# Causal attention before two feed-forward layers: the third and fourth unit's scores in one run, both value products behind them

## The chip, the cores and the metric

The kernel runs on one core of one Trainium2 chip. Its time is the device time of one execution in microseconds. Three runs of the kernel before gave 975.97, 975.77 and 975.14 us, median 975.77 us. A profile, taken in a run of its own, is where all readings below come from.

## The reference

An attention with a causal mask and a bias that only decays (4 batches, 8 heads, 576 positions, head size 64) feeds two feed-forward layers (2304 tokens, width 512, inner width 2048). All in float32; the inputs are scaled so that single-pass products would not do.

```python
scores = scale * np.matmul(q, k.transpose(0, 1, 3, 2))      # 4 x 8 heads, 576 x 576
cum = np.cumsum(np.maximum(s, 0.0), axis=-1)
bias = -(cum[:, :, :, None] - cum[:, :, None, :])
scores = np.where(causal, -1e9, scores + np.minimum(bias, 0.0))
attn = np.exp(scores - scores.max(-1, keepdims=True))
attn = attn / (attn.sum(-1, keepdims=True) + 1e-09)
x = np.matmul(attn, v)                                       # -> 2304 x 512
h = x @ w_in;  x = np.maximum(0.01 * h, h) @ w_out           # first layer
h = x @ w2_in; out = softplus(h) @ w2_out                    # second layer
```

## The kernel before

Two heads that lie side by side in the 128 partitions make a **pair**; there are 16 pairs (0 to 15), four to a batch. A pair is cut into four **units** of score rows, in this order: the first unit is rows 384 to 511 of both heads (512 keys each), the second the 64 last rows of both heads ("last" in the code, two stretches of 288 keys), the third rows 256 to 383 (384 keys), the fourth rows 128 to 255 and 0 to 127 (256 and 128 keys). A loop over 64 + 3 **steps** runs them: step i (0 to 3) of a pair is written as `p, i = divmod(n, 4)`, and in it `u0` is the unit whose softmax starts, `u1` the one before it, `u2` the one before that. For a unit the stations are

- scores on TensorE (`scores`, L311 and, for the second unit, L297), one step ahead of its own: `start(n + 1)`. They use half of the array's rows for each head. They fill a bank of PSUM for each half (tags `s0` and `s1`, two banks each, so units take turns);
- in its own step maxima on VectorE (`maxima`, L332) and exponentials on ScalarE (`exps`, L344), first half `j = 0`, second half `j = 1`;
- one step later the sums' reciprocals on VectorE (L350, L351) and the scaling on GpSimd (`norm`, L355);
- two steps later the transposes on TensorE (`transpose`, L372, L367, L363; three or four of 128 x 128 in a half) into one of two banks (tag `t`), and the copies out of them (`evacuate`, L384 on ScalarE, L386 on VectorE) to the tiles PA, PZ and PB. A transpose waits for the copy out of the bank two halves earlier.

The second product (`pv`, L403) of pair p - 1 stands in pair p: at the end of step 0 that for its rows 384 to 575, a bank with 192 columns out of PA and PZ; at the end of step 2 that for rows 0 to 383, out of PB. It uses half of the array's columns for each head. Its result is split in two parts, `xh` on ScalarE (L410) and `xl` on VectorE (L414).

Between these stand **fill units**: pieces of the first feed-forward layer for a batch that is done, to give TensorE work while the softmax runs. A fill unit is twelve matmuls of 512 columns with the whole array (L145 or L614), six in one step and six in the next, into a single bank (tag `m`). When the twelve are done, ScalarE copies them out of the bank (L587 or L618, written at the end of the second step), and the next unit's first matmul waits for that. From pair 7 to pair 10 a fill unit begins in steps 0 and 2; step 0 of pair 11 has none, and from there on they begin in steps 1 and 3 (step 1 of pair 15 has none). The weights for it are prepared in the same steps (`split_w`: two copies on ScalarE at L108 and L109, then L114, L117, L120 on VectorE, L123 on GpSimd, L127 on ScalarE, L133 on GpSimd).

All engines work through their instructions in the order in which the program writes them; `later(k, f)` writes f after k ticks, with one tick in the middle and one at the end of each step. The attention ends at about 240 us; what follows is the two feed-forward layers alone.

Of the kernel before, what the change touches and what calls it, by code (L numbers as in the profile page):

```python
# [10 lines left out]
F32 = mybir.dt.float32  # L11
# [3 lines left out]
AF = mybir.ActivationFunctionType  # L15
ALU = mybir.AluOpType
PSUM = bass.MemoryType.PSUM

P = 128
# [12 lines left out]
def attn_moe_moe(ctx, tc, q, k, v, s, w1i, w1o, w2i, w2o, out):  # L32
    nc = tc.nc

    B, H, S = s.shape
    D = v.shape[-1]
# [5 lines left out]
    NPAIR = H // 2  # L42
# [26 lines left out]
    def later(n, fn, *args):  # L69
        todo.setdefault(clock[0] + n, []).append((fn, args))  # L70
# [84 lines left out]
    def attention(att, ps, fills):  # L155
# [232 lines left out]
        def pv(p, last):  # L388
# [12 lines left out]
            for m, (c, x, o, w) in enumerate(mms):  # L401
                for j in range(2):
                    nc.tensor.matmul(  # L403
                        pt[j * D:(j + 1) * D, o:o + w], V[p % 2][:, c, j, :], x[:, j, :],
                        start=m == 0 or (not last and m == 1), stop=m == len(mms) - 1 or (not last and m == 0),
                    )
            c = slice(b * S + q0, b * S + q0 + n)

            def high():
                nc.scalar.activation(xh[:, hp, c], pt[:, :n], AF.Copy)  # L410
                later(1, low)

            def low():
                nc.vector.tensor_tensor(xl[:, hp, c], pt[:, :n], xh[:, hp, c].bitcast(F32), op=ALU.subtract)  # L414
                if not last and hp == NPAIR - 1 and b < B - 1:
                    fill.ready(b)

            later(1, high)

        mask = att.tile([P, NB * P], F32, tag="mask", name="mask")  # L420
        maskl = att.tile([P, S // 2], F32, tag="maskl", name="maskl")
# [33 lines left out]
        order = [[NB - 1], [], [NB - 2], [1, 0]]  # L455
        units = [(p, ts) for p in range(NP) for ts in order]
        live = {}

        def start(n):
            if n < len(units):  # L460
                live[n] = Unit(*units[n])
                live[n].scores()

        start(0)
        for n in range(len(units) + 3):
            p, i = divmod(n, len(order))
            u0, u1, u2, u3 = (live.get(n - d) for d in range(4))
            if u3:
                u3.evacuate(1)
            start(n + 1)  # L470
            if u0:
                u0.maxima(0)
                u0.exps(0)
            if u1:
                u1.divisors()
                u1.norm(0)
            if u2:
# [12 lines left out]
                fill.step(n)  # L490
            if u0:
                u0.maxima(1)
            if u2 and u0 and u0.last:
                u2.evacuate(0)
            if u0:
                u0.exps(1)
# [7 lines left out]
            if u1:  # L504
                u1.norm(1)
            if u2:
                if not (u0 and u0.last):
                    u2.evacuate(0)
                u2.transpose(1)
            if i == 3 and p + 1 < NP:  # L510
                load(p + 1, "v")
            elif i in (0, 2) and p:
                pv(p - 1, i == 0)
            if n >= len(units):
                fill.run()
# [335 lines left out]
```

## Time and profile before

| | |
|---|---|
| median of three runs | 975.77 us |
| the profiled execution | 976.11 us |
| its span in the trace | 974.3 us |
| TensorE (PE) busy | 967.0 us, 5268 matmuls |
| weight loads (PEld) busy | 785.0 us |
| VectorE (DVE) / ScalarE (ACT) / GpSimd (POOL) busy | 529.3 / 536.1 / 576.2 us |
| chain that ended last | PE 97% |
| PE in its chain at L311, L403, L372 | 5%, 4%, 4% |
| granted TensorE clock | 9 (0.9 or more) in each of the forty slices |

The profile's own time is 1.8 us longer than its span, and 0.34 us above the median of the runs. Times in the rows below are microseconds from the start of the span. A matmul row gives the start and the length of a merged group; the ends are modelled and overlap, so differences are taken from start to start. A float32 matmul shows as two records (two passes), and the two heads' matmuls start 0.007 us apart and run side by side in their halves of the array.

### The profile page before, as it was taken

The numbers are of one execution on the slowest core, as the hardware profiler recorded it, in microseconds if no ns is written. First come the engines' busy times: TensorE is split into PE (matmuls) and PEld (weight loads), VectorE is DVE, ScalarE is ACT, GpSimd is POOL, SyncE is SP. The second block draws the span as 40 slices with busy tenths as digits, with TensorE's granted clock in tenths as the row PEclk, the third lists the DMA queues.
The fourth block names the chain that finished last, engine by engine and source line by source line (L and its number), as shares of the span: only waits on it lengthen the run. The fifth ranks groups of instructions, "written<-read, shape, count | busy, mean of one in ns | idle before, by whom it ended". The sixth has DMA issues, their size and how long they took to land.

```text
span 974.3 us, 14738 instructions
## 1 busy us (share of the span) xinstructions
PE 967.0 (99%) x5268; PEld 785.0 (81%) x5268; DVE 529.3 (54%) x1140; ACT 536.1 (55%) x1119; POOL 576.2 (59%) x568
## 2 busy tenths in 40 slices
PE   9999999999999999999999999999999999999998
PEld 6666777777998888888888888888888888888886
DVE  7888566554122222222325358666688868764434
ACT  6888677565453333333344456766656655654452
POOL 7788556443454444344535556777677767774554
PEclk9999999999999999999999999999999999999999
DMA  6444452420621111111102110211011101100202
GB/s 230 156 160 140 134 170 77 143 73 23 218 85 43 44 44 43 35 52 44 44 23 65 44 44 22 65 39 48 22 44 45 64 23 44 44 0 1 87 22 87
DMA packets 37774, 68.06 MB, mean 70 GB/s; under 512 B 3018, under 2 KB 20298, under 8 KB 37700
## 3 DMA queue, kind: packets, MB, share of 16 engines
q1 hardware_dynamic: 37268, 66.36, 21.2%
q8 instruction: 42, 0.69, 0.3%
q10 hardware_dynamic: 432, 0.75, 0.2%
q14 instruction: 32, 0.26, 0.1%
HBM read 59.01 MB, written 8.09 MB: 69 GB/s over the span
## 4 chain that ended last, share of the span: by engine, by line
PE 97%; DVE 1%; POOL 1%; ACT 0%; issue 0%; DMA 0%; DVEq 0%; POOLq 0%
PE ps_h L145 41%; PE ps_out L752 37%; PE pt_s L311 5%; PE pt_v L403 4%; PE pt_t L372 4%; PE ps_o L614 3%; PE pt_t L367 1%; PE pt_s L297 1%; PE pt_w L191 0%; POOL sc L355 0%; DVE sc L332 0%; POOL wil L133 0%; DVE acc L764 0%; DVE PA L386 0%; ACT sc L344 0%
## 5 line engine op out<-in xcount | busy, mean ns | idle before, releaser
L151 POOL TENSOR_TENSOR gl<-gf,gh 128x512 fp32r<-128x512 f32 (+2 forms) x148 | 182.6, 1234 | 150.5 <-ACT gh L150 140.8
L145 PE MATMUL ps_h<-xh,wih 128*128 128x512 f32 (+2 forms) x640 | 237.5, 371 | 0.0
L145 PE MATMUL ps_h<-xh,wil 128*128 128x512 f32 (+2 forms) x640 | 235.8, 368 | 0.0
L145 PE MATMUL ps_h<-xl,wih 128*128 128x512 f32 (+2 forms) x640 | 235.6, 368 | 0.0
L764 DVE TENSOR_TENSOR acc<-ps_out,acc 128x512 f32<-128x512 f32 (+1 forms) x115 | 73.8, 657 | 164.2 <-PE ps_out L752 164.2
L711 POOL TENSOR_TENSOR t<-e,t 128x512 f32<-128x512 f32 (+1 forms) x80 | 112.2, 1403 | 72.2 <-DVE t L710 71.4
L355 POOL TENSOR_SCALAR sc<-sc,st 128x512 f32<-128x512 f32 (+4 forms) x160 | 89.0, 567 | 82.7 <-DVE st L351 76.2
L145 PEld LDWEIGHTS ps_h<-xh,wil 128*128 128x128 f32 x640 | 120.5, 188 | 19.7
L145 PEld LDWEIGHTS ps_h<-xh,wih 128*128 128x128 f32 x640 | 120.6, 188 | 19.3
L145 PEld LDWEIGHTS ps_h<-xl,wih 128*128 128x128 f32 x640 | 120.6, 189 | 19.1
L695 ACT ACTIVATE gf<-ps_h 128x512 f32<-128x512 f32 (+2 forms) x68 | 37.3, 548 | 177.4 <-PE ps_h L145 174.6
L150 ACT ACTIVATE gh<-gf 128x512 fp32r<-128x512 f32 (+2 forms) x148 | 86.1, 582 | 49.1 <-DVE gf L721 48.5
L752 PE MATMUL ps_out<-woh,gl 128*128 128x512 f32 x289 | 112.5, 389 | 0.0
L752 PE MATMUL ps_out<-wol,gh 128*128 128x512 f32 x289 | 112.4, 389 | 0.0
L752 PE MATMUL ps_out<-woh,gh 128*128 128x512 f32 x289 | 112.4, 389 | 0.0
L123 POOL TENSOR_TENSOR wm<-wm,wt 128x512 int32<-128x512 int32 x64 | 85.2, 1332 | 30.7 <-DVE wm L120 30.7
L344 ACT ACTIVATE sc<-sc,st 128x512 f32<-128x512 f32 (+2 forms) x144 | 83.4, 583 | 31.4 <-DVE st L350 20.1
L752 PE MATMUL ps_out<-gh,wol 128*128 128x512 f32 (+2 forms) x272 | 99.1, 364 | 0.0
L752 PE MATMUL ps_out<-gh,woh 128*128 128x512 f32 (+2 forms) x272 | 99.1, 364 | 0.0
L752 PE MATMUL ps_out<-gl,woh 128*128 128x512 f32 (+2 forms) x272 | 99.0, 364 | 0.0
L710 DVE TENSOR_SCALAR t<-e 128x512 f32<-128x512 f32 (+1 forms) x80 | 44.2, 552 | 98.2 <-ACT e L701 98.2
L114 DVE TENSOR_SCALAR wm<-wm 128x512 f32<-128x512 f32 x64 | 38.1, 596 | 92.7 <-ACT wm L108 92.6
(112 smaller groups left out, 1677.1 us busy)
## 6 DMA issues: line engine op xcount, KB each, us to landing
rawi<-in_moe_w_in SPq DMA_DIRECT2D x32, 512.0 KB
rawo<-in_moe_w_out SPq DMA_DIRECT2D x32, 512.0 KB
K<-in_k SPq DMA_DIRECT2D x15, 432.0 KB
V<-in_v SPq DMA_DIRECT2D x16, 320.0 KB
Q<-in_q SPq DMA_DIRECT2D x15, 320.0 KB
out<-acc SPq DMA_DIRECT2D x17, 256.0 KB
M<-c_d SPq DMA_DIRECT2D x30, 144.0 KB
part<-o SPq DMA_DIRECT2D x12, 256.0 KB
```

Of the source, the lines that this page charges most:

```text
L123: nc.gpsimd.tensor_tensor(m, m, t, op=ALU.add)
L145: nc.tensor.matmul(ps, a, b, start=kk == 0 and n == 0, stop=kk == KD - 1 and n == 2)
L150: nc.scalar.activation(gh, gf, AF.Copy)
L151: nc.gpsimd.tensor_tensor(gl, gf, gh.bitcast(F32), op=ALU.subtract)
L311: nc.tensor.matmul(self.ps[j][:, c], x[r, t * P:(t + 1) * P], y[r, :(t + 1) * P], start=x is Q[i], stop=x is bq,)
L344: nc.scalar.activation(x, x, AF.Exp, scale=-1.0, bias=self.stat(0, e + self.last), accum_out=self.stat(1, e))
L355: nc.gpsimd.tensor_scalar(x, x, self.stat(2, e), 1.0, op0=ALU.mult, op1=ALU.mult)
L372: nc.tensor.transpose(pt[:, c * P:(c + 1) * P], sc[:, j, c * P:(c + 1) * P], ident)
L710: nc.vector.tensor_scalar(t, e, 1.0, -1.0, op0=ALU.add, op1=ALU.add)
L711: nc.gpsimd.tensor_tensor(t, e, t, op=ALU.subtract)
L752: nc.tensor.matmul(u, a, v, start=f == 0 and m == 0, stop=f == G - 1 and m == 2 and j == k - 1)
L764: nc.vector.tensor_tensor(d[..., x], o[..., x], d[..., x], op=ALU.add)
```

## The change

From pair 7 to pair 15 the second step's `start(n + 1)` is left out: the third unit's scores are issued at the head of step 2, and the fourth unit's right behind them. Behind these stands `pv2`, which does both second products of pair p - 1 in one run: first the one out of PB, then the one out of PA and PZ. Its 576 columns don't fit a bank of 512, so each matmul of 192 columns is parted into one of 128 (same bank as the rest) and one of 64, which goes to free columns of the third unit's score bank. The two products at the end of steps 0 and 2 are gone for these pairs. `finish` writes the two parts of the result: for the 64 columns L414 and L421 of the new file at the end of step 2, for the other 512 in one instruction each, ScalarE's at the end of step 2 and VectorE's in the middle of step 3. In step 2 the second unit's reciprocals and first scaling now come before the third unit's maxima; in step 0 the copy out of the third unit's first transposes (`evacuate(0)`) now comes before the exponentials of the second half. For each pair 26 matmul instructions take the place of 18 in the second product.

```diff
--- before.py
+++ after.py
@@ -404,18 +404,42 @@
                         pt[j * D:(j + 1) * D, o:o + w], V[p % 2][:, c, j, :], x[:, j, :],
                         start=m == 0 or (not last and m == 1), stop=m == len(mms) - 1 or (not last and m == 0),
                     )
+            finish(p, pt[:, :n], q0, n, 1, not last)
+
+        def finish(p, pt, q0, n, wait, end):
+            b, hp = divmod(p, NPAIR)
             c = slice(b * S + q0, b * S + q0 + n)
 
             def high():
-                nc.scalar.activation(xh[:, hp, c], pt[:, :n], AF.Copy)
-                later(1, low)
+                nc.scalar.activation(xh[:, hp, c], pt, AF.Copy)
+                if n == TL:
+                    low()
+                else:
+                    later(1, low)
 
             def low():
-                nc.vector.tensor_tensor(xl[:, hp, c], pt[:, :n], xh[:, hp, c].bitcast(F32), op=ALU.subtract)
-                if not last and hp == NPAIR - 1 and b < B - 1:
+                nc.vector.tensor_tensor(xl[:, hp, c], pt, xh[:, hp, c].bitcast(F32), op=ALU.subtract)
+                if end and hp == NPAIR - 1 and b < B - 1:
                     fill.ready(b)
 
-            later(1, high)
+            later(wait, high)
+
+        def pv2(p, rest):
+
+            pt = ps.tile([P, 512], F32, tag="a", name="pt_v", bufs=1)
+            q3, qt = pt[:, SB - P:], rest[:, SB - P:SB - P + TL]
+            mms = [(0, PB[:, :, 2, :P], pt[:, :P], True, True)] + [
+                (c, PB[:, :, c, max(0, c - 1) * P:], pt[:, max(c, 1) * P:SB - P], c == 0, c == NB - 2)
+                for c in range(NB - 1)
+            ]
+            for c in range(NB):
+                mms += [(c, PA[:, :, c, :P], q3, c == 0, c == NB - 1), (c, PA[:, :, c, P:], qt, c == 0, False)]
+            mms.append((NB, PZ, qt, False, True))
+            for c, x, y, a, z in mms:
+                for j in range(2):
+                    nc.tensor.matmul(y[j * D:(j + 1) * D], V[p % 2][:, c, j, :], x[:, j, :], start=a, stop=z)
+            finish(p, qt, SB, TL, 2, False)
+            finish(p, pt, 0, SB, 2, True)
 
         mask = att.tile([P, NB * P], F32, tag="mask", name="mask")
         maskl = att.tile([P, S // 2], F32, tag="maskl", name="maskl")
@@ -455,9 +479,10 @@
         order = [[NB - 1], [], [NB - 2], [1, 0]]
         units = [(p, ts) for p in range(NP) for ts in order]
         live = {}
+        wide = 7
 
         def start(n):
-            if n < len(units):
+            if n < len(units) and n not in live:
                 live[n] = Unit(*units[n])
                 live[n].scores()
 
@@ -467,11 +492,21 @@
             u0, u1, u2, u3 = (live.get(n - d) for d in range(4))
             if u3:
                 u3.evacuate(1)
-            start(n + 1)
+            late = wide <= p < NP
+            if late and i == 2:
+                start(n)
+                u0 = live[n]
+            if not late or i != 1:
+                start(n + 1)
+            if late and i == 2:
+                pv2(p - 1, u0.ps[0])
+            if u1 and late and i == 2:
+                u1.divisors()
+                u1.norm(0)
             if u0:
                 u0.maxima(0)
                 u0.exps(0)
-            if u1:
+            if u1 and not (late and i == 2):
                 u1.divisors()
                 u1.norm(0)
             if u2:
@@ -490,7 +525,8 @@
                 fill.step(n)
             if u0:
                 u0.maxima(1)
-            if u2 and u0 and u0.last:
+            soon = u2 and u0 and (u0.last or late and i == 0)
+            if soon:
                 u2.evacuate(0)
             if u0:
                 u0.exps(1)
@@ -504,12 +540,12 @@
             if u1:
                 u1.norm(1)
             if u2:
-                if not (u0 and u0.last):
+                if not soon:
                     u2.evacuate(0)
                 u2.transpose(1)
             if i == 3 and p + 1 < NP:
                 load(p + 1, "v")
-            elif i in (0, 2) and p:
+            elif i in (0, 2) and p and not late:
                 pv(p - 1, i == 0)
             if n >= len(units):
                 fill.run()
```

TensorE, pair 13, from the third unit's second transposes (step 0) to the first fill matmul of step 1, before. The rows name line, operation, result and operands, the shape, and the engines waited for.

```order
L372 MATMUL pt_t<-ident,sc 128x128 [waits DVE_49,Pool_49]
L372 MATMUL pt_t<-ident,sc 128x128 x2
L403 MATMUL pt_v<-PA,V_97 64x192 [waits DMAHW5_49]
L403 MATMUL pt_v<-PA,V_97 64x192 x7
L403 MATMUL pt_v<-PZ,V_97 64x64 x2
L311 MATMUL pt_s<-K_88,Q_86 128x384 [waits DVE_49] x2
L311 MATMUL pt_s<-BK_92,BQ_90 128x384 x2
L372 MATMUL pt_t<-ident,sc 128x128 [waits Activation_49,Pool_49]
L372 MATMUL pt_t<-ident,sc 128x128
L372 MATMUL pt_t<-ident,sc 128x128 [waits Pool_49]
L145 MATMUL ps_h<-xh,wih 128x512 [waits Activation_49]
```

The same stretch after:

```order
L372 MATMUL pt_t<-ident,sc 128x128 [waits DVE_49,Pool_49]
L372 MATMUL pt_t<-ident,sc 128x128 x2
L372 MATMUL pt_t<-ident,sc 128x128 [waits Activation_49,Pool_49]
L372 MATMUL pt_t<-ident,sc 128x128
L372 MATMUL pt_t<-ident,sc 128x128 [waits Pool_49]
L145 MATMUL ps_h<-xh,wih 128x512 [waits Activation_49]
```

The second product (L403) and the third unit's scores (L311) are gone from between the two groups of three transposes, so the fourth unit's first transposes (they wait for ScalarE and GpSimd) and the fill's first matmul (it waits for ScalarE) follow at once.

TensorE, pair 13, the end of step 1 and the head of step 2, before:

```order
L372 MATMUL pt_t<-ident,sc 128x128 x3
L311 MATMUL pt_s<-K_88,Q_86 128x256 x2
L311 MATMUL pt_s<-BK_92,BQ_90 128x256 x2
L311 MATMUL pt_s<-K_88,Q_86 128x128 x2
L311 MATMUL pt_s<-BK_92,BQ_90 128x128 x2
L372 MATMUL pt_t<-ident,sc 128x128 x4
```

The same place after, up to the second matmul of 64 columns:

```order
L372 MATMUL pt_t<-ident,sc 128x128 x3
L311 MATMUL pt_s<-K_88,Q_86 128x384 x2
L311 MATMUL pt_s<-BK_92,BQ_90 128x384 x2
L311 MATMUL pt_s<-K_88,Q_86 128x256 x2
L311 MATMUL pt_s<-BK_92,BQ_90 128x256 x2
L311 MATMUL pt_s<-K_88,Q_86 128x128 x2
L311 MATMUL pt_s<-BK_92,BQ_90 128x128 x2
L440 MATMUL pt_v<-PB,V_97 64x128 x2
L440 MATMUL pt_v<-PB,V_97 64x256 x4
L440 MATMUL pt_v<-PB,V_97 64x128 x2
L440 MATMUL pt_v<-PA,V_97 64x128 x2
L440 MATMUL pt_s<-PA,V_97 64x64 x2
```

The third unit's scores (384 columns) have come behind the transposes, next to the fourth unit's, and the product out of PB and then PA follows them.

ScalarE, pair 13, step 0 and the head of step 1, before: exponentials of the first unit, copy out of the third unit's transposes, copy of the fill unit.

```order
L344 ACTIVATE sc,st<-sc,st 128x512 [waits DVE_49,PE_49]
L344 ACTIVATE sc,st<-sc,st 128x512 [waits DVE_49]
L384 ACTIVATE PB<-pt_t 128x3x128 [waits PE_49]
L618 ACTIVATE o<-ps_o 128x512 [waits DMAHW6_49,PE_49]
L410 ACTIVATE xh<-pt_v 128x192 [waits PE_49]
L384 ACTIVATE PB<-pt_t 128x3x128 [waits PE_49]
```

The same after:

```order
L344 ACTIVATE sc,st<-sc,st 128x512 [waits DVE_49,PE_49]
L384 ACTIVATE PB<-pt_t 128x3x128 [waits PE_49]
L344 ACTIVATE sc,st<-sc,st 128x512 [waits DVE_49]
L654 ACTIVATE o<-ps_o 128x512 [waits DMAHW6_49,PE_49]
L384 ACTIVATE PB<-pt_t 128x3x128 [waits PE_49]
```

The copy to PB moved ahead of the second exponential, and L410 is gone; the copy that frees the fill's bank (L618, now L654) stands third before and after it.

ScalarE, pair 12, the same place after:

```order
L344 ACTIVATE sc,st<-sc,st 128x512 [waits DVE_49,PE_49]
L384 ACTIVATE PB<-pt_t 128x3x128 [waits PE_49]
L344 ACTIVATE sc,st<-sc,st 128x512 [waits DVE_49]
L127 ACTIVATE woh<-wm 128x512 [waits Pool_49]
L654 ACTIVATE o<-ps_o 128x512 [waits DMAHW7_49,PE_49]
L384 ACTIVATE PB<-pt_t 128x3x128 [waits PE_49]
```

Here L127 of the weights' preparation, which waits for GpSimd, stands before the copy that frees the fill's bank, as it did before.

## Rows read from the trace of the kernel before

**Rows 1.** The page, busy time of each engine, share of the span, instructions.

```profile
PE 967.0 (99%) x5268; PEld 785.0 (81%) x5268; DVE 529.3 (54%) x1140; ACT 536.1 (55%) x1119; POOL 576.2 (59%) x568
```

**Rows 2.** Timeline of PE, pair 13: start, length, line, tiles, shapes, count.

```profile
190.12 0.49 PE L372 MATMUL pt_t<-ident,sc 128*128 128x128 f32 x3
190.54 1.52 PE L403 MATMUL pt_v<-PA,V 128*64 128x192 f32 x16
191.89 0.28 PE L403 MATMUL pt_v<-PZ,V 128*64 128x64 f32 x4
192.10 0.92 PE L311 MATMUL pt_s<-K,Q 64*128 64x384 f32 x4
192.56 0.64 PE L311 MATMUL pt_s<-BK,BQ 64*128 64x384 f32 x2
193.12 0.55 PE L372 MATMUL pt_t<-ident,sc 128*128 128x128 f32 x3
193.43 0.47 PE L145 MATMUL ps_h<-xh,wih 128*128 128x512 f32 x1
...
195.32 0.70 PE L311 MATMUL pt_s<-K,Q 64*128 64x256 f32 x4
195.67 0.47 PE L311 MATMUL pt_s<-BK,BQ 64*128 64x256 f32 x2
195.97 0.39 PE L311 MATMUL pt_s<-K,Q 64*128 64x128 f32 x4
196.11 0.31 PE L311 MATMUL pt_s<-BK,BQ 64*128 64x128 f32 x2
196.35 0.66 PE L372 MATMUL pt_t<-ident,sc 128*128 128x128 f32 x4
...
198.76 1.52 PE L403 MATMUL pt_v<-PB,V 128*64 128x128 f32 x16
...
200.21 1.13 PE L311 MATMUL pt_s<-K,Q 64*128 64x512 f32 x4
```

**Rows 3.** Timeline of PE, second pass of the last product matmuls of that pair.

```profile
191.94 0.23 PE L403 MATMUL pt_v<-PZ,V 128*64 128x64 f32 x2
```

**Rows 4.** Timeline of all engines, step 0 of pair 13 (in brackets: idle before, releaser).

```profile
187.80 0.28 DVE L386 COPY PZ<-pt_t 64x128 f32<-64x128 f32 x1 [0.81 <-PE pt_t L363]
...
188.78 0.72 ACT L344 ACTIVATE sc<-sc,st 128x512 f32<-128x512 f32 x1 [1.64 <-DVE st L350]
...
189.17 0.92 POOL L355 TENSOR_SCALAR sc<-sc,st 128x256 f32<-128x256 f32 x2 [3.87 <-DVE st L351]
...
190.05 0.72 ACT L344 ACTIVATE sc<-sc,st 128x512 f32<-128x512 f32 x1 [0.45 <-DVE st L332]
...
190.65 0.56 DVE L386 COPY PB<-pt_t 128x384 f32<-128x384 f32 x1 [0.63 <-PE pt_t L372]
...
190.77 0.47 ACT L384 ACTIVATE PB<-pt_t 128x384 f32<-128x384 f32 x1
...
191.14 0.58 ACT L618 ACTIVATE o<-ps_o 128x512 f32<-128x512 f32 x1
```

**Rows 5.** Timeline of ACT and PE in step 0 of pairs 9, 11 and 12.

```profile
127.32 0.66 ACT L108 ACTIVATE wm<-rawo 128x512 f32<-128x512 f32 x1
...
159.11 0.61 ACT L592 ACTIVATE gh<-gf 128x512 fp32r<-128x512 f32 x1
...
174.22 0.49 PE L372 MATMUL pt_t<-ident,sc 128*128 128x128 f32 x3
...
175.47 0.63 ACT L127 ACTIVATE woh<-wm 128x512 fp32r<-128x512 f32 x1
```

**Rows 6.** Timeline of PE and POOL in step 0 of pair 7.

```profile
95.93 0.49 PE L372 MATMUL pt_t<-ident,sc 128*128 128x128 f32 x3
...
96.04 0.92 POOL L355 TENSOR_SCALAR sc<-sc,st 128x256 f32<-128x256 f32 x2 [0.43 <-DVE st L351]
...
98.46 2.17 POOL L355 TENSOR_SCALAR sc<-sc,st 128x256 f32<-128x256 f32 x4
```

## The prediction

> **What bounds the kernel now.** I read the page's busy times first: TensorE is busy 967.0 of 974.3 us [rows 1], so anything that saves TensorE time, or makes it wait, shows in the end. Then the stretch that the change touches, the attention from pair 7 on, as a timeline of TensorE for one whole pair [rows 2]. The reader is to see two things there. No row carries an idle time: each group starts when the one before lets it, so a pair's length is set by TensorE alone. And the array's layout changes often (whole array for transposes and fill; half the rows per head for scores; half the columns per head for the second product), and each change costs something. Then the other engines in step 0 [rows 4]: they have pauses, but their work hangs on TensorE's (the row at 187.80 was released by a transpose at L363), and it has a fixed length. In the kernel before, 2.6 us of TensorE work, the first product and the third unit's scores (190.54 to 193.12 [rows 2]), lie between the point where step 0 ends on TensorE and the point where it needs what those engines make. The change takes this cover away. So I price both sides.
>
> **What TensorE saves in a pair.** Prices of a layout change first. Leaving: the last pass of 64 columns starts at 191.94 [rows 3] and the next group at 192.10, 0.16; a pass of 64 columns takes 191.94 - 191.89 = 0.05 [rows 2, 3], so leaving costs 0.10. Entering scores: the pair's K, Q matmuls take 0.46 to the next row with 384 columns and 0.35 with 256, thus 0.11 for each 128; with 128 columns that would be 0.24, but the one at 195.97, which follows scores, took 0.14 (196.11 - 195.97) [rows 2]: 0.10. Entering the second product: eight passes of 192 columns take 191.89 - 190.54 = 1.35, at three times the 64-column pass (0.055) 1.32; I take 0.05, for the transposes too.
>
> - Scores. Before 193.12 - 192.10 = 1.02 and 196.35 - 195.32 = 1.03 [rows 2]. In one run they lose one leaving and one entering: 0.20 saved.
> - Second product. Before 192.10 - 190.54 = 1.56 and 200.21 - 198.76 = 1.45 [rows 2]. In one run 0.10 + 0.05 less: 0.15 saved.
> - Transposes. The three at 190.12 took 0.42 because another layout followed; now transposes follow, 0.10 saved. The three at 193.12 came out of scores; now they don't, 0.05 saved.
>
> Together 0.50 of a pair's TensorE time. Nine pairs: **4.5 us**. Nothing else on TensorE changes in number but the eight instructions more: 192 columns parted into 128 and 64. Eight passes of 64 columns a pair cost nothing if each takes its 0.05 and the rest the other 0.11. If their weight loads don't keep up they take at most twice that, as a pass of 128 does: 8 x 0.05 = 0.4 a pair, 3.7 us. I take zero, since the pass from 191.89 to 191.94 [rows 3] had its successor's weights in time.
>
> The Trainium skill, "TensorE: Matmul & The Clock Gate", Part 3 (What overlaps and what doesn't), says that a weight load overlaps with running matmuls only where the row group differs. The halves here differ in columns only. By that rule each pass would show its load; the eight passes of 192 columns at 1.35 us don't, but no run here shows a row of 64-column passes between others.
>
> **What hides the rest.** The fourth unit's last transposes are copied by VectorE (0.56, as at 190.65 [rows 4]) while the scores run (1.02 + 1.03 - 0.20 = 1.85 [rows 2]), so the product finds them. The new wait of the next pair's first scores, for VectorE's read of the 64 columns, has four transposes, six fill matmuls and four transposes as cover (198.76 - 196.35 = 2.41 [rows 2]); behind the first of these come ScalarE's copy (0.58), the 64 columns (under 0.47) and VectorE's part (under 0.56) [rows 4], after 0.66 [rows 2]: 2.27 at most. It holds, by little. Queues of loads (SP, GpSimd) keep their order; the load of V waits for the product, which ends earlier. The two result instructions per product are as many as before, with the same columns.
>
> **What waits instead.** In step 0 nothing changes up to 190.12 [rows 2]. Then the fourth unit's first transposes are wanted at 190.12 + 0.32 = 190.44, the fill of step 1 at 190.44 + 0.25 = 190.69 (before: 193.12 and 193.43). What they need, in pair 13's clock:
>
> - Scaling by GpSimd: first tile at about 189.6, second 190.09 [rows 4]. In time.
> - The copy out of the transposes' bank: now right behind the first exponential, at 188.78 + 0.72 = 189.50, done 189.97 [rows 4]. In time here.
> - The fill's bank, where a fill unit begins in step 1 (pairs 12 to 14): ScalarE frees it behind the second exponential, which VectorE's maxima hold until 190.05: 190.05 + 0.72 + 0.58 = 191.35 [rows 4]. TensorE waits 0.7. **Pairs 13 and 14: 0.7 each.**
> - Pair 12: L127 stands ahead of that copy and can't run before 175.47, since it waits for GpSimd; it delays the copy to 176.01 at the soonest, done 176.6. Wanted: 174.22 + 0.57 = 174.8 [rows 5]. **1.8.**
> - Pair 11, no fill in step 0: the transposes come 1.47 sooner (fill to transposes, as 195.32 - 193.43 = 1.89 less the 0.42), at 189.0 in pair 13's clock; ScalarE has L592 (0.61, less the 0.1 by which neighbours overlap, 190.77 + 0.47 against 191.14) ahead of the copy [rows 4, 5], so it is done at 190.5. **1.5.**
> - Pair 9: two copies of the weights' preparation (0.66 and the like [rows 5]; 1.1 together, as they overlap by 0.1 each) ahead of the copy: done at 191.1, wanted 190.44. **0.7.** Pair 10: L592 ahead, done 190.5: **0.1.** Pair 8: nothing.
> - Pair 15, no fill in step 1: the fourth unit's second transposes are wanted at 190.44 + 0.33 = 190.77, the bank's copy by VectorE ends at 190.65 + 0.56 = 191.21 [rows 4]. **0.5.**
> - Pair 7: wanted 95.93 + 0.32 = 96.25; GpSimd ends the second tile at 96.96, needed for the third transpose 0.2 later: 0.5. The second transposes are wanted at about 98.6, but their scaling starts only at 98.46 and takes two tiles (0.92 for a pair of tiles) [rows 6]: 0.6. **1.1.**
>
> Sum 7.1 us of waits against 4.5 us saved: **2.6 us longer**. The profiled execution would take 976.11 + 2.6 = 978.7; the runs' median is 0.34 below that execution, so 978.4.
>
> **The rivals.**
>
> 1. Covers hold: the same work on ScalarE and VectorE starts earlier, because the longer step 2 gives those engines time, and the waits vanish. Time 975.8 - 4.5 = 971.3. For it: ScalarE is busy 55% only [rows 1]. Against: step 0's chain starts at L363 [rows 4], and time to spare in step 2 doesn't move that. Decides: whether the copy L654 in pairs 13 and 14 ends before 190.69 of the old clock. 15%.
> 2. Half the waits: my wanted times are too early, or one wait covers another; 3.6 of 7.1, time 975.8 - 4.5 + 3.6 = 974.9. 20%.
> 3. The 64-column passes are held by weight loads (the skill's rule above): 2.6 + 3.7, time 982.1. For it: nobody ran them in a row here; against: [rows 3]. 8%.
> 4. The run doesn't come together: the fourth unit's scores wait for VectorE to free their bank, so that the array drains between and 0.20 of the saving goes, 1.8 us in all: 980.2. Against: VectorE's second maxima follow the first copy at 191.2 [rows 4] by about an us, and the scores are wanted three us after 190.12. 7%.
>
> **How the numbers follow.** The forecast (50%) is 978.4, 2.6 longer. A measurement of this kernel can tell about 0.2%, 2.0 us, from no change: faster means below 973.8, slower above 977.7. Rival 1 is faster, rival 2 is the same, the forecast and rivals 3 and 4 are slower, but of the forecast's half about a tenth of all lies below 977.7, since each of the nine waits is known to some 0.15. So faster 15%, the same 29%, slower 56%. The range, 8 in 10: down to 973.5, which leaves rival 1 out; up to 981.5, which leaves out rival 3 and takes in rival 4. The forecast alone: 976.8 to 980.
>
> **What would show it.** Right: the timeline of TensorE has the second product once in a pair, 2.86 long; idle times appear before the fourth unit's transposes (L372) in pairs 7, 9, 11, released by ScalarE or GpSimd, and before the fill's first matmul in pairs 12 to 14, released by ScalarE's L623 or L654; in pair 8 the length of a pair is about 15.4 against 15.9. Wrong: 64-column passes more than 0.06 apart, no idle before the fill, or an idle of the next pair's first scores on VectorE's L421.

## The result, and the profile after

The changed kernel takes **987.61 us** (median of four runs, 987.55 to 989.71) against 975.75 us of the kernel before on the same chip: 1.0128 times as long, 95% interval 1.0113 to 1.0143, 11.9 us slower. The forecast was 978.4 us, in a range that ended at 981.5. The sign was right, the size was not: 2.6 us were expected and 11.9 came. The profiled execution's span went from 974.3 to 985.8 us.

The page of the changed kernel, busy times of the engines and the shares of the chain that ended last (it answers [rows 1]):

```profile
PE 964.4 (98%) x5412; PEld 787.3 (80%) x5412; DVE 529.0 (54%) x1140; ACT 534.0 (54%) x1119; POOL 574.9 (58%) x568
PE 92%; DVE 3%; ACT 2%; issue 1%; POOL 1%; DMA 0%; DVEq 0%; POOLq 0%; ACTq 0%
```

TensorE is busy 2.6 us less than before (967.0 in [rows 1]) in a span 11.5 us longer: idle time is up by 14.1 us. TensorE's share of the chain has fallen from 97% to 92%, and VectorE and ScalarE, which had 1% of it between them, have 5% now. So TensorE saved something and waited for much more. The waits of the changed kernel, TensorE's alone (line, released by, us in total, times, longest):

```profile
PE pt_s L311 <- issue: 4.5, 3, 1.7
PE pt_s L311 <- PE pt_t L372: 3.0, 5, 0.6
PE pt_t L372 <- ACT PB L384: 2.1, 2, 1.4
PE ps_o L650 <- ACT o L654: 1.8, 1, 1.8
PE pt_t L372 <- POOL sc L355: 1.7, 6, 0.4
...
PE ps_h L145 <- ACT o L654: 0.5, 1, 0.5
PE ps_h L145 <- ACT gf L623: 0.5, 1, 0.5
```

The last five are the forecast's own waits: transposes of the fourth unit for ScalarE's copy to PB and for GpSimd's scaling (three of these six, 0.9 us together, lie in pairs 7 and 15; the others were there before), and the fill's first matmul for ScalarE's copy out of its bank. The first two are others: L311, the scores, waits eight times, 7.5 us together. The timeline of TensorE shows where; it is pair 7 of the changed kernel, from its second product on (it answers the last rows of [rows 2]):

```profile
100.70 1.52 PE L440 MATMUL pt_v<-PB,V 128*64 128x128 f32 x16
102.06 0.39 PE L440 MATMUL pt_v<-PA,V 128*64 128x128 f32 x4
102.27 0.28 PE L440 MATMUL pt_s<-PA,V 128*64 128x64 f32 x4
102.39 0.39 PE L440 MATMUL pt_v<-PA,V 128*64 128x128 f32 x4
...
103.61 0.65 PE L372 MATMUL pt_t<-ident,sc 128*128 128x128 f32 x4
...
105.50 0.60 PE L372 MATMUL pt_t<-ident,sc 128*128 128x128 f32 x4
106.69 0.70 PE L311 MATMUL pt_s<-K,Q 64*128 64x512 f32 x2 [0.59 <-PE pt_t L372]
```

The next pair's first scores start 1.19 us after the four transposes at 105.50, where 0.53 is what such four take when nothing waits. In pairs 9, 10 and 11 the same place loses 1.71, 1.18 and 1.78 us. In the prediction's words this is "the new wait of the next pair's first scores", of which it said that it "holds, by little". What those scores wait for is VectorE's read of the 64 columns. The row names a transpose as releaser, and the three long waits name "issue", which is time in which the engine waited for nothing that the profile shows. The other engines' rows tell more. VectorE and ScalarE in the same stretch of the changed kernel:

```profile
103.84 0.56 DVE L332 CUSTOM_DVE_ANT_0 sc<-pt_s,mask 128x384 f32<-128x384 f32 x1 [4.06 <-PE pt_s L440]
...
104.32 0.55 DVE L332 CUSTOM_DVE_ANT_0 sc<-pt_s,mask 128x384 f32<-128x384 f32 x1
104.44 0.62 ACT L344 ACTIVATE sc<-sc,st 128x384 f32<-128x384 f32 x1 [4.75 <-DVE st L332]
...
105.05 0.60 ACT L344 ACTIVATE sc<-sc,st 128x384 f32<-128x384 f32 x1
...
105.65 0.57 ACT L384 ACTIVATE PA<-pt_t 128x512 f32<-128x512 f32 x1
106.13 0.21 ACT L414 ACTIVATE xh<-pt_s 128x64 fp32r<-128x64 f32 x1
...
106.37 0.23 DVE L421 TENSOR_TENSOR xl<-pt_s,xh 128x64 fp32r<-128x64 f32 x1 [1.49 <-ACT xh L414]
```

The first row is the whole story. VectorE has been idle for 4.06 us, and the third unit's maxima (L332) are released by **L440, the second product**, not by L311. The product's last matmuls write 64 columns into the bank that holds the third unit's scores, the maxima are written behind them in the program, and so the program makes them wait for all that is written to that bank before them. ScalarE then has both exponentials to do before it reaches the copy to PA (105.65) and the 64 columns (106.13); VectorE reads them at 106.37, and at 106.69 the scores follow.

### The profile page after: what moved, and what is told of

Its sections match the earlier page's. It is cut to its first block, busy times and chain, and to the rows that moved or that the text cites. A ratio compares the mean times of both kernels' runs of the same rounds, so it can differ in the third digit from the quotient of the medians.

```text
span 985.8 us, 15039 instructions
## 1 busy us (share of the span) xinstructions
PE 964.4 (98%) x5412; PEld 787.3 (80%) x5412; DVE 529.0 (54%) x1140; ACT 534.0 (54%) x1119; POOL 574.9 (58%) x568
## 4 chain that ended last, share of the span: by engine, by line
PE 92%; DVE 3%; ACT 2%; issue 1%; POOL 1%; DMA 0%; DVEq 0%; POOLq 0%; ACTq 0%
PE ps_h L145 40%; PE ps_out L788 36%; PE pt_s L311 5%; PE pt_t L372 3%; PE ps_o L650 2%; PE pt_v L440 2%; PE pt_v L403 2%; DVE sc L332 1%; ACT sc L344 1%; PE pt_t L367 1%; POOL sc L355 1%; PE pt_s L440 1%; PE pt_s L297 0%; DMA sc<-in_s 0%; DVE PA L386 0%
## 5 line engine op out<-in xcount | busy, mean ns | idle before, releaser
L355 POOL TENSOR_SCALAR sc<-sc,st 128x512 f32<-128x512 f32 (+4 forms) x160 | 88.8, 566 | 88.7 <-DVE st L351 75.4
```

The lines of the kernel that those rows point to most:

```text
L355: nc.gpsimd.tensor_scalar(x, x, self.stat(2, e), 1.0, op0=ALU.mult, op1=ALU.mult)
```

## The experiments

Theory A: the 64 columns' bank holds the third unit's maxima back, this costs some 7.5 us, and what is left of the loss is the waits that were forecast. Against it: the loss is all lost cover in steps 0 and 1 (B), or the read of the 64 columns holds the bank by itself (C), or the parted product costs (D). To compare runs I take the length of a pair, from the start of its first unit's scores (L311, 512 columns) to the start of the next pair's, out of TensorE's timeline of each run. All in us:

| pair | before | the change | maxima first | other bank | second half's bank | products only | scores only | bank first | copies first | put together |
|---|---|---|---|---|---|---|---|---|---|---|
| 7 | 14.67 | 16.11 | 15.45 | 15.45 | 15.44 | 15.14 | 14.49 | 15.46 | 14.67 | 14.49 |
| 8 | 16.09 | 16.14 | 15.42 | 15.42 | 15.42 | 15.80 | 15.87 | 15.42 | 15.62 | 15.61 |
| 9 | 15.90 | 18.01 | 16.27 | 16.27 | 16.28 | 15.80 | 15.71 | 16.27 | 15.44 | 15.44 |
| 10 | 15.89 | 16.85 | 15.67 | 15.67 | 16.16 | 15.79 | 15.67 | 15.67 | 15.45 | 15.45 |
| 11 | 14.50 | 17.43 | 15.64 | 15.65 | 15.65 | 15.33 | 14.32 | 15.65 | 15.62 | 14.31 |
| 12 | 15.90 | 18.14 | 19.15 | 19.15 | 19.17 | 16.76 | 15.84 | 15.84 | 15.85 | 15.86 |
| 13 | 15.90 | 16.84 | 16.17 | 16.15 | 16.20 | 15.80 | 15.71 | 15.72 | 15.77 | 15.71 |
| 14 | 15.89 | 16.87 | 16.15 | 16.17 | 16.18 | 15.79 | 15.67 | 15.76 | 15.73 | 15.68 |
| sum, less before's 124.74 | | +11.65 | +5.18 | +5.19 | +5.76 | +1.47 | -1.46 | +1.05 | -0.59 | -2.19 |
| median time | 975.7 | 987.61 | 980.85 | 979.65 | 980.65 | 977.15 | 974.06 | 976.57 | 974.88 | 973.36 |

The pairs are read from the profiled execution, the median is that of all executions. With the maxima first, the other bank and the second half's bank, pair 12 holds 1.7 us of a fall of TensorE's clock, which the median of the other bank's executions seems to be without (last section); so the sum is above the difference of the medians there (5.19 against 4.0).

**The maxima first.** The maxima are written before the product, so that they wait for the scores alone.

```diff
-            if late and i == 2:
-                pv2(p - 1, u0.ps[0])
...
             if u0:
                 u0.maxima(0)
+            if late and i == 2:
+                pv2(p - 1, u0.ps[0])
+            if u0:
                 u0.exps(0)
```

> The third unit's first maxima (L332) are written ahead of the product run instead of behind it; each engine keeps the order of its instructions, the 64 columns stay in the third unit's score bank, only what the maxima wait for changes. Theory A (the maxima wait for the last product matmul into their bank, about 4 us late, and that delays the exponentials, the copies out of the transposes' banks and the 64 columns' read, which TensorE then waits for): the maxima start right behind the scores, the idle times at the next pair's first scores (0.66 us in pairs 7, 8, 12 to 14, 1.1 to 1.7 us in the three pairs with weight preparation, 7.5 us in all) fall under 0.2 each, and the time goes from 987.6 to about 980 (978.5 to 982), still slower than before by the waits in steps 0 and 1. Theory B (the loss is all lost cover in steps 0 and 1, the late maxima lie beside other work): no change, 986.5 to 988.5. Theory C (the read of the 64 columns, L421, holds the bank by itself, wherever the maxima stand): the idle times at the first scores stay, 986 or more.

Measured: 980.85 us, 1.0048 times before (1.0033 to 1.0063). Theory A holds, B and C fall: 6.8 us went with the instructions in the same order on each engine, and from pair 7 on L311 no longer stands among TensorE's waits. What is left is led by these, from the waits of this run:

```profile
PE pt_t L372 <- ACT PB L384: 2.1, 2, 1.4
PE ps_o L651 <- ACT o L655: 1.9, 1, 1.9
```

**The other bank.** The 64 columns go to the fourth unit's bank, whose maxima come a step later.

```diff
-                pv2(p - 1, u0.ps[0])
+                pv2(p - 1, live[n + 1].ps[0])
```

> The 64 columns go to the free columns of the fourth unit's score bank, nothing else. The third unit's maxima then wait for its scores alone, and the read of the 64 columns holds a bank that is wanted only by the next pair's second unit, four matmul groups later. Theory A: as with the maxima first, about 980 (978 to 982), at most 0.5 us below that run. Theory B: 986.5 to 988.5. Theory C: about 980 here, and 986 or more with the maxima first.

Measured: 979.65 us, 1.0039 times before (1.0025 to 1.0054), pair by pair the same as with the maxima first. Pair 7 of this run, the same rows of VectorE, ScalarE and TensorE:

```profile
100.11 0.56 DVE L332 CUSTOM_DVE_ANT_0 sc<-pt_s,mask 128x384 f32<-128x384 f32 x1 [0.30 <-PE pt_s L311]
...
104.33 0.60 ACT L384 ACTIVATE PA<-pt_t 128x512 f32<-128x512 f32 x1 [2.31 <-PE pt_t L372]
...
105.08 0.22 DVE L421 TENSOR_TENSOR xl<-pt_s,xh 128x64 fp32r<-128x64 f32 x1 [3.92 <-ACT xh L414]
...
106.07 0.70 PE L311 MATMUL pt_s<-K,Q 64*128 64x512 f32 x2
```

The maxima are released by L311 and start 3.7 us earlier (100.11 against 103.84), ScalarE's copy to PA waits for its transposes and for nothing else, and the 64 columns have been read (105.30) 0.8 us before the scores start.

**The second half's bank.** A dose between: the columns stay with the third unit, in the bank of its second head.

```diff
-                pv2(p - 1, u0.ps[0])
+                pv2(p - 1, u0.ps[1])
```

> A dose between the change and the run with the other bank: the 64 columns go to the third unit's second score bank (that of its second head) in place of its first, all else as in the change. Theory A: the first maxima (L332) start behind the scores, only the second ones wait for the product's end; the chain behind that (maxima, exponentials, copy to PA, 64 columns, VectorE's read) is one exponential shorter, 0.61 us (pair 7 of the changed kernel: 104.44 to 105.05). So the 0.66 us at the next pair's first scores go in pairs 7, 8 and 12 to 14, and in pairs 9 to 11 some 0.6 of 1.71, 1.18 and 1.78 goes: 987.6 - 3.4 - 1.8, about 982.4 (981 to 984), between the change (987.6) and the other bank (979.65). Theory C (only the read of the 64 columns holds a bank): 986 or more.

Measured: 980.65 us, 1.0046 times before (1.0031 to 1.0062), below the expected range. By the medians it is far better than the change, but can't be told from the other bank: the executions took 979.57 to 981.96 us here and 979.12 to 981.01 there. The pairs show the order that A has (one half free is better than none and worse than both), at a lower price than I expected: only pair 9's end still waits, 0.48 (in the table it counts to pair 10, 16.16 against 15.67). The reason is in ScalarE's rows. In pair 9 of the changed kernel:

```profile
137.55 0.62 ACT L344 ACTIVATE sc<-sc,st 128x384 f32<-128x384 f32 x1 [4.66 <-DVE st L332]
...
138.16 0.61 ACT L628 ACTIVATE gh<-gf 128x512 fp32r<-128x512 f32 x1
138.68 0.60 ACT L344 ACTIVATE sc<-sc,st 128x384 f32<-128x384 f32 x1
...
139.28 0.57 ACT L384 ACTIVATE PA<-pt_t 128x512 f32<-128x512 f32 x1
139.76 0.62 ACT L127 ACTIVATE woh<-wm 128x512 fp32r<-128x512 f32 x1
140.28 0.20 ACT L414 ACTIVATE xh<-pt_s 128x64 fp32r<-128x64 f32 x1
```

What stands between the two exponentials (L628 here; the weights' L108 and L109 in pair 11) also moves into the wait when the first one is free. So the chain is shorter by 138.68 - 137.55 = 1.13 in pair 9, and by 173.48 - 171.75 = 1.73 in pair 11, instead of 0.61. And these rows explain why pairs 9 to 11 lose more than the others: fill work and weight preparation (L127 at 139.76) stand in ScalarE's queue between the late maxima and the 64 columns.

**Products only.** The third unit's scores back in step 1; the product in one run, 64 columns in the fourth unit's bank.

```diff
-            if not late or i != 1:
-                start(n + 1)
+            start(n + 1)
             if late and i == 2:
-                pv2(p - 1, u0.ps[0])
+                pv2(p - 1, live[n + 1].ps[0])
```

> One part alone: both products in one run at the head of step 2, 64 columns in the fourth unit's bank, but the third unit's scores stay in step 1 as before the change. Theory A with my prices: 0.25 us saved in each of nine pairs (0.15 in the product, 0.10 behind the transposes of step 0), 2.3 us; the cover of step 0 is 1.0 us instead of 2.6, so the fill's wait stays only in pair 12 (0.6) and the transposes' in pair 11 (0.3): about 974.5 (973.5 to 976). Theory B (any loss of cover in step 0 costs in full): 1.56 us less cover, 976 to 979. Theory D (the parted product itself costs: 64-column passes between 128-column ones): 978 to 982.

Measured: 977.15 us, 1.0014 times before (1.0005 to 1.0023), some 2.6 us above my expectation. A clean pair takes 15.80 against 15.90, so the run of both products saves 0.10, not 0.25: the transposes of step 0 are still followed by a change of layout, which I had counted as gone. The rest is waits that I hadn't listed, of the scores themselves. In pair 11 of this run, TensorE and VectorE:

```profile
158.43 1.52 PE L311 MATMUL pt_s<-K,Q 64*128 64x384 f32 x3
...
158.61 0.68 DVE L332 CUSTOM_DVE_ANT_0 sc<-pt_s,mask 128x512 f32<-128x512 f32 x1
...
159.78 0.48 PE L311 MATMUL pt_s<-K,Q 64*128 64x384 f32 x1
```

The last K, Q matmul starts 1.35 us after the first. My reading is that the second head's scores want the bank that VectorE's second maxima of the first unit are reading until 159.3, and that before the change the product stood in front and hid it; no row names a releaser here, and no run moves these maxima alone. The stretch from the first of these scores to the next transposes takes 1.94 us instead of 1.02, in pair 7 1.61. With pair 12's wait for the fill's bank (0.9) that is more than the eight pairs save. The time lies in theory B's range (976 to 979), but not by its mechanism: pairs 9, 10, 13 and 14 lost the same cover and got 0.10 shorter, and only pairs 7, 11 and 12 got longer. Theory D falls: the two products take 2.91 us, 0.1 less than before.

**Scores only.** Third and fourth unit's scores together, the products at their old places.

```diff
-            if late and i == 2:
-                pv2(p - 1, u0.ps[0])
...
-            elif i in (0, 2) and p and not late:
+            elif i in (0, 2) and p:
```

> The other part alone: the third unit's scores together with the fourth's at the head of step 2, both products at their old places, 192 columns in a pass. Theory A: 0.20 us saved in each of nine pairs, 1.8 us; the cover of step 0 is the product's 1.56 us, so hardly a wait (0.2 in pair 12), the third unit's maxima start 0.5 to 1 us later than before and that lies beside other work: about 974 (973.3 to 975.5). Theory B': starting the third unit's scores in its own step is what costs, as its softmax then ends too late for the transposes two steps on: 978 to 983.

Measured: 974.06 us, 0.9984 times before (0.9974 to 0.9993). It came as expected: 0.18 to 0.22 saved in seven of the eight pairs of the table (pair 12 waits 0.14 for the fill's bank, so 0.06 is left there). This part of the change is a gain by itself, and the late start of the third unit's softmax does no harm: theory B' falls.

**The fill's bank first.** On top of the other bank: in step 0, ScalarE's copy out of the fill's bank ahead of the second exponentials, and so ahead of L127 in pair 12.

```diff
             if soon:
                 u2.evacuate(0)
+            fill.release()
             if u0:
                 u0.exps(1)
...
-                later(1, leaky)
+                self.then(leaky)
...
-                later(1, store)
+                self.then(store)
```

`then` holds the copy (`leaky` or `store`, after the kind of fill unit) back in step 0 of the late pairs and `release` writes it.

> As with the 64 columns in the fourth unit's bank, and in step 0 of the late pairs ScalarE's copy out of the fill's bank is written ahead of the exponentials of the first unit's second half instead of behind them (and so ahead of the weights' preparation in pair 12). Theory A (what is left of the loss is what I forecast for steps 0 and 1: instructions ahead of the copies that TensorE waits for): the fill's waits in pairs 12 to 14 shrink from 1.86, 0.46 and 0.48 us of idle to under 0.3 each; in pair 12 also the half clock goes that the trace shows right behind the idle time (granted 0.50 for some 3.6 us, 1.7 us longer in matmul starts): 979.65 - 4.3, about 975.4 (974.3 to 976.5). Theory E (the clock's fall has another reason than this idle time): it stays, 977. Theory F (the exponentials that are put back make the next step wait instead): 978 or more.

Measured: 976.57 us, 1.0009 times before (1.0000 to 1.0018). Between the two profiled executions the spans differ by the expected 4.3 us (979.1, 974.8); the medians differ by 3.1, so that the time is just above theory A's range. I had read the 4.3 from a profiled execution with the fall of the clock and taken it from a median that seems to be without. Pairs 12, 13 and 14 got shorter by 3.31, 0.43 and 0.41 us, with 0.28 of wait left in each. The half clock went with the idle time (the mean granted clock is 0.999 or 1.000 in all ten executions): theory E falls. Both exponentials' results still come in time: theory F falls.

**The copies first.** On top of that, the copy out of the third unit's first transposes ahead of both exponentials, and the new order only from pair 8 on.

```diff
-        wide = 7
+        wide = 8
...
             if u0:
                 u0.maxima(0)
+            if early:
+                u2.transpose(0)
+                u2.evacuate(0)
+            if u0:
                 u0.exps(0)
```

> As the run before it, and the copy out of the third unit's first transposes is written ahead of the first unit's exponentials in step 0, and the new order begins with pair 8 instead of pair 7. Theory A: the waits of pairs 9, 10 and 11 (0.84, 0.22 and 1.70 us longer than a pair without waits) shrink to 0.3 in all; pair 7 takes its old 14.67 us instead of 15.45. Together 3.2 us less than the run before it: about 972.2 (971 to 973.5), faster than before the change. Theory F: the later exponentials delay the scaling on GpSimd, and the transposes two steps on wait for that: 975 or more.

Measured: 974.88 us, 0.9991 times before (0.9982 to 1.0000): a measurement can't tell it from no change. Pairs 9 and 10 came out clean (15.44 and 15.45), pair 11 didn't. From TensorE's timeline, pair 11 of this run:

```profile
157.12 0.68 PE L372 MATMUL pt_t<-ident,sc 128*128 128x128 f32 x3 [0.59 <-POOL sc L355]
159.47 0.68 PE L372 MATMUL pt_t<-ident,sc 128*128 128x128 f32 x3 [0.30 <-POOL sc L355]
```

Where TensorE waited for ScalarE's copy (1.42 in the changed kernel), it now waits for GpSimd's scaling of the fourth unit: one late thing took the place of another, in the step that has no fill to hide it. The time is 1.4 us above theory A's range, and in pair 11 it is theory F's mechanism that shows, though not at its full price (975 or more).

**Put together.** Scores together from pair 7 on, both products in one run only in pairs 8 to 10, where the cover holds, with the copies first there; the other pairs keep the products at their old places.

```diff
-        wide = 8
+        wide, joint = 7, (8, 9, 10)
...
-            if late and i == 2:
+            both = late and p in joint
+            if both and i == 2:
                 pv2(p - 1, live[n + 1].ps[0])
```

> A version put together from what the runs showed: scores of third and fourth unit together from pair 7 on (0.20 a pair, as with the scores alone), both products in one run only in pairs 8 to 10, where the pair took 15.62, 15.44 and 15.45 us with the copies first against 15.87, 15.71 and 15.67 with the scores alone; the other pairs keep the products at their old places. Theory A: 974.06 - 0.74, about 973.3 (972.6 to 974.2), faster than before by some 0.24%. Theory F (pairs don't add up, waits move to the pair where the order changes back): 974 to 976.

Measured: 973.36 us, **0.9976 times before (0.9968 to 0.9985)**: 2.4 us faster than before and 14.3 us faster than the change. Pair by pair it is what its parts were. Its page, busy times:

```profile
PE 964.8 (99%) x5316; PEld 786.5 (81%) x5316; DVE 528.6 (54%) x1140; ACT 535.9 (55%) x1119; POOL 575.6 (59%) x568
```

TensorE is busy 2.2 us less than in [rows 1], and this time the span follows (972.0 against 974.3).

**Put together, and earlier.** As this one, with the scores together from pair 5 and the products joined in pairs 5 and 6 too.

```diff
-        wide, joint = 7, (8, 9, 10)
+        wide, joint = 5, (5, 6, 8, 9, 10)
```

> As the run before it, with the scores together from pair 5 on and the products in one run in pairs 5 and 6 too. Pairs 5 and 6 of the kernel before took 15.88 and 15.90 us, as the clean pairs later, and with a clean cover each would lose 0.4: about 972.5 (971.8 to 974). Rival: VectorE and ScalarE are busier there (8 to 9 us of 10 each between 50 and 90 us of the kernel before, with the weights' preparation), so that the copies come late and TensorE waits: 974 to 977.

Measured: 975.73 us, 1.0001 times before (0.9992 to 1.0009). The rival's time came, but not by the engines that I had named: pairs 5 and 6 took 16.63 and 17.35 us, 0.75 and 1.45 longer than before instead of 0.4 shorter. TensorE's timeline of pair 6 says for whom:

```profile
85.17 0.44 PE L372 MATMUL pt_t<-ident,sc 128*128 128x128 f32 x2 [0.78 <-POOL sc L355]
```

GpSimd's scaling (L355) is late there, as in pairs 7 and 11; in this pair it stands behind L133 of the weights' preparation (from 82.59, 1.79 long) and starts at 84.63. In the kernel before, 2.6 us of product and scores stood between the transposes of step 0 and no wait shows; that they hid the same lateness is argued, no run was made to show it.

## Why the prediction was right and wrong

**What TensorE saves: right.** 0.50 a pair was forecast. A pair without waits is pair 8 with the other bank, 15.42 us, against 15.90 of a pair without waits before (pair 8 itself took 16.09 there): 0.48, for nine pairs 4.3 us (4.5 forecast). By parts, from start to start: scores 1.85 as forecast, against 2.05; both products 2.90 against 3.02 in that pair, 0.12 (0.15 forecast); transposes of step 0 0.57 against 0.72, 0.15 as forecast. The passes of 128 and of 64 columns alternate at 0.21 and 0.12 us for two passes each (102.06, 102.27, 102.39 above): 0.06 for 64 columns, no price for the weight loads. Rival 3 falls. The weight loads of the same passes in the changed kernel:

```profile
102.17 0.25 PEld L440 LDWEIGHTS pt_s<-PA,V 128*64 128x64 f32 x4
102.33 0.20 PEld L440 LDWEIGHTS pt_v<-PA,V 128*64 128x64 f32 x4
```

Each group of loads starts while the matmuls before it run: 102.17 lies between 102.06 and 102.27, 102.33 between 102.27 and 102.39. The sentence of the Trainium skill, "TensorE: Matmul & The Clock Gate", Part 3, that a load overlaps only where the row group differs, does not hold here, for halves of the array that differ in columns.

**What waits in steps 0 and 1: right in place, a little small.** The excess over a clean pair, from start to start in the changed kernel:

| pair | 7 | 8 | 9 | 10 | 11 | 12 | 13 | 14 | 15 | sum |
|---|---|---|---|---|---|---|---|---|---|---|
| forecast | 1.1 | 0 | 0.7 | 0.1 | 1.5 | 1.8 | 0.7 | 0.7 | 0.5 | 7.1 |
| measured | 1.23 | 0 | 0.87 | 0.22 | 1.70 | 2.05 | 0.76 | 0.77 | 0.6 | 8.2 |

Each is where it was forecast, and where the profile names a releaser it is the forecast one, but for pair 15 (GpSimd's scaling where I had VectorE's copy; its 0.6 is an estimate from the transposes of the other pairs, as no clean pair of its kind was run). Pairs 12 and 13, the fill's first matmul:

```profile
183.50 0.50 PE L650 MATMUL ps_o<-gh,woh 128*128 128x512 f32 x1 [1.77 <-ACT o L654]
...
200.35 0.50 PE L145 MATMUL ps_h<-xh,wih 128*128 128x512 f32 x1 [0.48 <-ACT o L654]
```

The bracket is smaller than the loss: in pair 13 it says 0.48 and the start is 0.7 late. The matmul before the wait has its full modelled length there, which overlaps the next one's when nothing waits. The forecast fell short for another reason. I had costed most waits up to the end of the copy, but TensorE starts a little later: in pair 13 the copy ends at 199.72 + 0.58 = 200.30 and the fill's matmul starts at 200.35, in pair 9 the copy ends at 129.16 + 0.47 = 129.63 and the transposes start at 129.78. What is left of the difference in pair 12 is GpSimd's, which released L127 later than forecast. Rivals 1 and 2 fall: the covers did not hold, and the waits were not halved. Rival 4 falls too: the scores came together, in 1.85.

**What hides the rest: this step failed.** "The new wait of the next pair's first scores [...] holds, by little" cost 8.0 us: 0.66, 0.72, 1.71, 1.18, 1.78, 0.66, 0.66 and 0.66 at the ends of pairs 7 to 14. I let the chain begin with ScalarE's copy to PA, 0.66 after the transposes start. That is when its data are ready, and with the other bank it does start then (103.64 to 104.33, 0.69); the whole chain from there to the end of VectorE's read takes 1.66 us in that run (to 105.30), within the 2.27 that I had allowed. In the changed kernel it takes 2.99 (103.61 to 106.60), more than the cover of 2.41. I didn't ask what stands ahead of the copy in ScalarE's queue, two exponentials, and what those wait for, the maxima; and I took it that the maxima wait for the scores, though the change writes the product into the maxima's bank ahead of them. I had seen that bank as a place that the next scores must wait for, and not as a place that its present reader must wait for. The rule is in the Trainium skill, "PSUM — Partial Sum Buffer", section "PSUM bank collisions raise a hardware error": accesses of two engines are to be ordered by bank (and quadrant of the partitions), not by address. The trace agrees that the program does so: the maxima read columns 0 to 383, the product's last matmuls write columns 384 to 447, and VectorE had been idle 4.06 us when L440 released the maxima. Whether the order is kept for the bank or for the tile no run here can tell, as each of these tiles has a bank to itself. The same page of the Trainium skill, in its section "Summary: rules for kernel authors", says to read a different bank from the one that a running matmul writes; that is what the run with the other bank did.

The sum, with the measured terms: 8.2 + 8.0 - 4.3 = 11.9 us; the spans differ by 11.5. The small rest is in the tail of the last pair (the profile shows 0.3 and 0.8 us of waits after 241 us, where before had 0.3 and 0.4) and in the stage ahead of the change, whose end varies by some 0.9 us from run to run (pair 7 starts at 90.58 in the changed kernel and at 91.36 before). That the sign was right is not luck: without the bank's wait, in the run with the other bank, the time is 979.65 us, 1.3 above the forecast and inside its range.

**What would show it.** The prediction named "an idle of the next pair's first scores on VectorE's L421" as a sign of its failure. That is what came, only that the row names other releasers. The signs of its being right came too, the waits in pairs 7, 9 and 11 to 14, but for pair 8: it took 16.14 us in the changed kernel, and 15.42 (15.4 forecast) only with the other bank.

## What to carry to other kernels

Free columns of a bank were not free here: whoever writes them ties his end to the start of whoever reads the rest of the bank behind him in the program. Take a bank whose reader comes late, or write the reader down first. When you check that a wait holds, follow the releasing engine's queue backwards, instruction by instruction, to the first one that waits for something the change moves; and when a change takes cover away in some places and not in others, make it only where the cover holds.

## What was not expected of the hardware

In pair 12, behind the wait for the fill's bank, TensorE's granted clock fell from 1.00 to 0.50 (1.2 GHz) for some 3.4 us in the profiled executions of three kernels: maxima first, other bank, second half's bank. By windows of the run with the other bank (from:to, length, busy times and instructions of PE, PEld, DVE, ACT, POOL, granted clock, busy share of the DMA engines, GB/s):

```profile
175.00:177.00 2.00, 0.68 (x7) 0.44 (x5) 1.54 (x8) 1.44 (x4) 2.00 (x4) 1.00 0.43 120
177.00:178.00 1.00, 0.46 (x2) 0.42 (x3) 0.17 (x2) 1.00 (x3) 1.00 (x3) 1.00 0.00 0
178.00:179.00 1.00, 1.00 (x5) 0.81 (x4) 0.00 (x0) 0.62 (x2) 1.00 (x2) 0.73 0.64 244
179.00:180.00 1.00, 1.00 (x5) 0.66 (x4) 0.00 (x0) 0.00 (x0) 1.00 (x2) 0.50 0.06 18
180.00:181.00 1.00, 1.00 (x4) 0.51 (x4) 0.60 (x2) 0.00 (x0) 0.00 (x0) 0.50 0.00 0
181.00:182.00 1.00, 1.00 (x8) 0.60 (x6) 0.18 (x2) 0.00 (x0) 0.59 (x2) 0.57 0.00 0
182.00:183.00 1.00, 1.00 (x16) 0.88 (x14) 0.71 (x3) 0.12 (x1) 0.39 (x1) 1.00 0.00 0
```

The fall comes a microsecond after TensorE has started again at 177.54, after 1.86 us of idle time, and costs more: pair 12 takes 19.15 us there and 18.14 - 0.66 = 17.48 in the changed kernel without the wait at its end, 1.7 us more, which is what 3.4 us at half clock cost. The changed kernel idled 1.77 us at the same place, and its clock stayed:

```profile
184.00:185.00 1.00, 1.00 (x5) 0.73 (x5) 0.00 (x0) 0.58 (x2) 1.00 (x2) 1.00 0.67 254
185.00:186.00 1.00, 1.00 (x10) 0.70 (x8) 0.47 (x1) 0.00 (x0) 0.97 (x2) 1.00 0.03 8
```

So a repair that took 8.0 us of waits away gave 1.7 back, in this execution, in a place that it hadn't touched. With the fill's bank first, the idle time and the fall are both gone (pair 12 at 15.84).

The kernel alone does not decide it. With the maxima first and with the other bank, four of the nine executions have a mean granted clock of 0.997 or 0.998, the profiled ones among them, and spans of 979.1 to 979.8 us; the other five have 1.000 and spans of 977.3 to 978.6. (With the second half's bank the four executions go from 0.997 to 1.000.) By an estimate from the windows above, 3.4 us at half clock lower the mean over 979 us by 0.002, so these five seem to have gone without the fall. Why 1.86 us of idle time brought it in some executions, and 1.77 us didn't in the changed kernel's profiled one, is open; no run here was made to tell.
